# A chunked recurrence in front of two dense layers: stores, copies and products of the run-up in other places

## Chip, cores, metric

One NeuronCore of one Trainium2 chip runs the whole program in one launch. The metric is the device time of one execution in microseconds (us), lower is better. All data are float32.

## What is computed

Six arrays r, k, v, w, a, b of shape batch 4, heads 8, sequence 768, width 40 drive a recurrence; each of the 32 (batch, head) pairs has a 40x40 state, zero at first. Its result goes through two dense layers:

```python
for t in range(S):
    y[:, :, t] = np.einsum('bhd,bhde->bhe', rt, state)
    Sa = np.einsum('bhde,bhe->bhd', state, at)
    state_decay = state * wt[:, :, None, :] - np.einsum('bhd,bhe->bhde', Sa, bt)
    state = state_decay + np.einsum('bhd,bhe->bhde', vt, kt)
# x = y as [4, 768, 320]
h = relu(x @ w_in); c = conv3_along_sequence(h, conv_w)      # d_ff 1024
x = (h * sigmoid(c)) @ w_out
h = relu(x @ w2_in); u, v = halves(h)                        # 512 each
out = (u * (w_spatial @ layernorm(v) + b_spatial)) @ w2_out
```

## The kernel before, in words

The recurrence is worked in blocks. The sequence is cut into six groups n = 0 to 5 of 128 steps, each of two chunks of 64. A unit kk (0 to 23) is one batch i in one group n; a pair p (0 to 11) is two batches of one group, so it holds units 2p and 2p+1. All loads are made by pairs. The third to sixth pair of the change are pairs 2 to 5.

**The decay.** `lam_prep(n)` (line 55) makes for groups n and n+1 the running products of w (`lam`, 40 scans forward on VectorE, line 73) and their reciprocals (`ilam`, a reciprocal and 40 scans backward, line 79). Both are stored to DRAM scratch (`put`, line 65, four stores per kind, 320 KB each) and read back pair by pair in another layout. `l0`, `l2` and `l4` are these generators for groups 0|1, 2|3 and 4|5. The source of the `ilam` of groups 2 and 3 lies in a buffer of the tag "G", which later holds a pair's G tile.

**Loading a pair.** `l_araw`, `l_ln`, `l_P`, `l_il` (lines 101 to 134) issue loads on SyncE's queue (SP): a, lam (tile `lnA`), the packed b|k (tile `P`) and ilam (tile `il`, two copies of 64x16x40 into the lower half; one buffer for most pairs). `l_g` (line 121) multiplies a by lam into the tail of the pair's G tile on GpSimd (POOL); `l_ar` (line 126) copies it to `AR` on ScalarE (ACT); `l_dup` (line 138) copies the lower half of `il` to the upper half on ACT; `l_pm` (line 145) multiplies `P` by `il` on VectorE (DVE). `loadZ` (line 310) loads v|r of a pair (tile `ZU`, three buffers shared with the decay tiles of `l0`, `l2` and `l4`), `loadV` (line 315) copies v from it on ACT.

**One unit.** `A(kk)` transposes `AR` (line 157, TensorE), masks it on ACT (`bdA`, 159), transposes `P` (167), copies that to `PT` on ACT (168), multiplies the two (174) and masks the result into G on DVE (175). When the second unit of a pair is done, G's diagonal blocks are stored to `tb` (181, four stores). `subst(n)` loads them as `L` (189), inverts them by substitution on DVE (198 to 208), copies the result to `LT` (211) and stores `dt` and `dd` (213, 214); `loadD(p)` loads these back (226, 227 or 229). `Bp(kk)` builds the inverse of the whole chunk (lines 244 to 296), `Cp(kk)` carries the state through both chunks (327 to 342), `Dp(kk)` makes the output (360 to 385).

**What sets the order.** The program is written out by hand for SP, DVE and ACT: each executes its instructions in the order in which the Python emits them. Ahead of the loop (lines 420 to 466) the emission is a plain list of calls. `mixed(kk,g,m)` emits A(kk) with m scans of the generator g in its middle; `steps(g,m)` emits m steps of a generator; `drain` the rest. `later(m,f)` puts f off by m ticks, `flush()` emits everything put off. In the loop, unit kk does its C and D, B of the next unit and A of the unit nine ahead in slots given by `ORDER`; each slot is a tick, and the table `SCHED` says in which slot the loads of a coming pair stand. The first pass (kk = 0) has offsets of its own (lines 497, 498). `L4T` is the tick at which the eight `lam` and `ilam` stores of groups 4 and 5 are emitted. The numbers of steps stand in `W`. After the recurrence come the two layers (lines 788 to 922), which the change leaves alone.

Of the kernel before, what the change touches and what calls it, by code (L numbers as in the profile page):

```python
# [11 lines left out]
def attention(tc, keep, ident, vr,bk,w,a, x, spare=None):  # L12
# [4 lines left out]
    with ExitStack() as ctx:  # L17
# [36 lines left out]
        lms={}; BQ=[sy]  # L54
# [32 lines left out]
        def later(m,f):  # L87
            due.append((now[0]+m,f)); 
# [4 lines left out]
        def flush():  # L93
            while due: tick()
# [6 lines left out]
        def l_araw(p):  # L101
            if p>=NK//2: return
            n,j,u,s0,bs,xs=part(p)
            t=u['a']=sb.tile([128,H2,D],F32,name="araw",tag="VM",bufs=6) if p<4 else sb.tile([128,H2,D],F32,name="araw",bufs=1)
            sy.dma_start(out=t,in_=a[n,j])
# [5 lines left out]
        def l_P(p):  # L111
            if p>=NK//2: return
            n,j,u,s0,bs,xs=part(p)
            P=u['P']=sb.tile([128,H2,2,D],F32,name="P",bufs=6)
            sy.dma_start(out=P,in_=bk[n,j].rearrange("q t x c e -> (q t) x c e"))
        def l_g(p):
            if p>=NK//2: return
            n,j,u,s0,bs,xs=part(p)
            u['AR']=sb.tile([64,H2,2,D],F32,name="AR",bufs=2)
            G=u['G']=keep.tile([128,H2,2*C+D],F32,name="G",bufs=5)  # L120
            G_.tensor_tensor(G[:,:,2*C:],u['a'],u['lnA'],ALU.mult)
        def l_ar(p):
            if p>=NK//2: return
            n,j,u,s0,bs,xs=part(p)
            for c in range(2):
                AC.copy(u['AR'][:,:,c],u['G'][c*C:(c+1)*C,:,2*C:])
            u['ok1']=True
# [7 lines left out]
        def l_dup(p):  # L135
            if p>=NK//2: return
            n,j,u,s0,bs,xs=part(p)
            AC.copy(u['il'][64:128],u['il'][0:64])
            u['ok3']=True
        def l_pm(p,eng=None):  # L140
            if p>=NK//2: return
            n,j,u,s0,bs,xs=part(p)
            assert u['ok3']
            for hs in (slice(0,H),slice(H,H2)) if p==0 else (slice(0,H2),):
                (eng or G_).tensor_tensor(u['P'][:,hs],u['P'][:,hs],u['il'][:,:,hs].rearrange("p c h e -> p h c e"),ALU.mult)
            u['ok2']=True
# [256 lines left out]
        def drain(g):  # L403
            for _ in g: pass
# [4 lines left out]
        with tc.manual_schedule(engines={mybir.EngineType.SP,mybir.EngineType.DVE,mybir.EngineType.Activation}):  # L409
            flat=lambda t: t.rearrange("p h e -> p (h e)")[:,0:512]  # L410
            def both(g,f):

                for _ in g:
                    yield
                    next(f,None)
            def steps(g,m):
                for _ in range(m): next(g,None)
            def mixed(kk,g,m):
                A_=A(kk); steps(A_,3); steps(g,m); drain(A_)
            l0=lam_prep(0); next(l0); next(l0)  # L420
            il12={p:sb.tile([128,2,H2,D],F32,name="il2",tag="P",bufs=6) for p in (1,2)}
            l_araw(0); l_P(0)
            l2=lam_prep(2); next(l2); next(l2)
            steps(l0,D+1); lms['lam',0](); l_P(1)
            l_ln(0); l_ln(1); l_araw(1)
            l_g(0); l_ar(0); l_g(1)
            drain(l0); lms['ilam',0]()
            l_il(0); l_il(1)
            lms['lam',1](); lms['ilam',1]()
            warm(flat(pair[0,0]['lnA']),WARM0); warm(flat(pair[0,1]['lnA']),WARM1)  # L430
            l_ar(1); l_dup(0)
            l_P(2); l_araw(2); l_ln(2); l_il(2)
            steps(l2,W[0]); l_pm(0,V)
            a0=A(0); next(a0); warm(flat(pair[0,1]['lnA']),WARM2)
            steps(a0,2); l_dup(1); steps(l2,W[1]); drain(a0)
            l_pm(1,V)
            mixed(1,l2,W[2]); flush()
            lam_end(0)
            l4=lam_prep(4); next(l4); next(l4)
            mixed(2,l2,W[3]); mixed(3,l2,W[4]); flush()  # L440
            s0=subst(0); next(s0)
            l_P(3); l_araw(3); l_ln(3); l_il(3)
            l_g(2); l_ar(2); l_dup(2)
            drain(l2); l_pm(2,V)
            mixed(4,l2,0); steps(l4,W[11])
            steps(s0,W[5])
            mixed(5,s0,W[6]); flush()
            lms['lam',2](); lms['lam',3]()
            drain(s0); flush()
            loadD(0)  # L450
            loadZ(0); lms['ilam',2]()
            l_g(3); l_dup(3); l_ar(3); steps(l4,W[7]); l_pm(3,V)
            mixed(6,l4,W[8]); mixed(7,l4,W[8])
            l_P(4); l_araw(4); l_ln(4); flush()
            sub1=subst(1); next(sub1)
            lms['ilam',3](); l_il(4)
            b0=Bp(0)
            for _ in range(4): next(b0); steps(l4,W[9])
            loadV(0)
            drain(b0); drain(l4)  # L460
            later(7,lambda: (l_g(4),l_ar(4),l_dup(4))); later(10,lambda: l_pm(4,V))
            bg.append(sub1)
            def l4done():
                for f in ('lam','ilam'):
                    for z in (4,5): lms[f,z]()
            later(L4T,l4done)
            with tc.manual_schedule():
                none=iter(()); acc=0.0; dg={}
                def staging(z):
                    def tmp():  # L470
                        mo=sb.tile([128,2,512],F32,name="mo",tag="bdA",bufs=1)
                        return [sb.tile([128,512],I32,name="ct",tag="PT",bufs=2),mo[:,0],mo[:,1]]
                    return (lambda: sb.tile([128,512,2],I32,name="raw",tag="AR",bufs=2)),tmp
                later_layer=spare(FC=512,staging=staging) if spare else none
                done=0
                ex=lambda kk: EX[kk-14] if kk>=14 else 0
                for kk in range(NK):
                    i,n=units[kk]
                    ahead=[z for z in (EARLY[kk] if kk<len(EARLY) else [kk+LA] if kk+LA<NK-2 or not LAST2 else [NK-2,NK-1] if kk+LA==NK-2 else []) if z<NK]
                    gens={'A':chain(*[A(z) for z in ahead]),'B':Bp(kk+1) if kk+1<NK else none,'C':Cp(kk),'D':dg.pop(kk-1) if kk else none}  # L480
                    gens['Z']=dg[kk]=Dp(kk)
                    if kk==6 or kk==14: lam_end(n+1)
                    po=(kk+LA)//2 if (kk+LA+1)%2 else (kk+LA+1)//2
                    z=-1
                    for g in ORDER if kk<TAIL else ORDER2:
                        if g=='W':
                            warm(ident,WM)
                            continue
                        z+=1
                        for _ in range(max(1,len(ahead)) if g=='A' else 1): next(gens[g],None)  # L490
                        if z in BX and kk+1<NK and units[kk+1][1] in SMALL: next(gens['B'],None)
                        while done<ex(kk-1)+(ex(kk)-ex(kk-1))*(z+1)//19:
                            next(later_layer,None); done+=1
                        tick(); acc+=RATE0 if kk<3 else RATE if kk<14 else RATE2; pump(int(acc)); acc-=int(acc)
                        for s,f in SCHED[(kk+LA+1)%2]+SCHEDC[kk%2]:
                            if s==z:
                                if f=='il' and kk==0: later(12,lambda po=po: l_il(po))
                                elif f=='Z' and kk==0: later(18-z,lambda kk=kk: loadZ(kk//2+1))
                                elif f=='Z': loadZ(kk//2+1)
                                elif f=='V': loadV(kk//2+1)  # L500
                                else: {'araw':l_araw,'ln':l_ln,'P':l_P,'g':l_g,'ar':l_ar,'il':l_il,'pm':(lambda p: l_pm(p,V)) if PMV else l_pm,'dup':l_dup}[f](po)
                    if any(z%4==3 for z in ahead): nxt=subst(ahead[-1]//4 if ahead[-1]%4==3 else ahead[0]//4); ll=LL if kk+LA<NK-2 else LL2; later(ll,lambda z=nxt: next(z)); later(ll+SUB,lambda z=nxt: bg.append(z))
                pump(1000)
                for _ in dg.pop(NK-1): next(later_layer,None)
                flush()
# [5 lines left out]
ORDER2="DCCDDBCBACDADDABBAA"  # L511
ORDER="CDCBDDCBDDACABBDAAA"
LA=9
L4T=4
RATE=1.25
RATE2=1.25
RATE0=1.4
# [13 lines left out]
SMALL=(0,)  # L531
BX=(0,9)
DTLS=2
W=[34,9,9,12,12,8,8,12,8,9,4,10]
EX=[3, 7, 7, 9, 11, 15, 19, 22, 26, 28]


# [527 lines left out]
```

## Time and profile before

| | us |
|---|---|
| median of 3 runs | 969.81 |
| lowest, highest | 964.55, 976.65 |
| the profiled execution | 971.86 |
| its span, first to last instruction | 970.1 |

The rows further down come from the profiled execution; times in them are microseconds from the start of its span. A row of the timeline has the start, the duration, the engine, the source line, the operation, what it writes and reads, how many instructions are merged in it, and in square brackets how long the engine was idle before and what ended that. PE is the matmul side of TensorE. SPq rows are the issue of a DMA, not its transfer. PEclk is the granted TensorE clock as a share of 2.4 GHz, so 0.50 is 1.2 GHz.

### The profile page before, as it was taken

How to read it: one execution, taken by the hardware profiler on the slowest of the kernel's cores; microseconds unless marked ns; L12 is line 12 of the kernel's file. 1: busy time of each engine (PE TensorE's matmuls, PEld its weight loads, DVE VectorE, ACT ScalarE, POOL GpSimd, SP SyncE). 2: the span in 40 equal slices, each digit the busy share in tenths (PEclk: the TensorE clock that was granted, in tenths of full speed). 3: DMA queues.
4: the chain of work that ended last, by engine and by line, in shares of the span. 5: the costliest groups of instructions: out<-in, count | busy, mean ns of one | idle time of the engine just before them, and what ended most of it. 6: DMA issues, size and time to landing. Idle time of an engine off the chain costs nothing. (4 is left out here: it accounts for less than half of the span.)

```text
span 970.1 us, 23472 instructions
## 1 busy us (share of the span) xinstructions
PE 869.4 (90%) x9575; PEld 799.8 (82%) x9575; DVE 662.0 (68%) x1503; ACT 535.8 (55%) x1166; POOL 204.2 (21%) x268
## 2 busy tenths in 40 slices
PE   0876579999999999989988889998999999998997
PEld 0565569899998998888877779997899889998997
DVE  6876738387695886866659977368743877268841
ACT  0452547777778776457756655266534654266521
POOL 2100000111112102023320011234222441234321
PEclk9975669999999999779979899999999999999999
DMA  9978773555745537144331230111011100011001
GB/s 217 206 163 188 206 156 73 153 109 114 163 112 144 119 73 177 40 127 122 96 103 54 85 105 8 45 51 46 1 32 55 34 22 25 22 51 31 1 2 45
DMA packets 149189, 86.70 MB, mean 89 GB/s; under 512 B 124176, under 2 KB 138256, under 8 KB 147152
## 3 DMA queue, kind: packets, MB, share of 16 engines
q1 hardware_dynamic: 148800, 84.78, 35.2%
q8 instruction: 77, 1.26, 0.5%
q14 instruction: 40, 0.33, 0.1%
q10 hardware_dynamic: 272, 0.33, 0.1%
HBM read 61.24 MB, written 23.86 MB: 88 GB/s over the span
## 5 line engine op out<-in xcount | busy, mean ns | idle before, releaser
L688 PE MATMUL psp<-spt,vv 128*128 128x384 f32 x576 | 105.6, 338 | 0.5 <-DVE vv L816 0.3
L688 PE MATMUL ph<-XT,G 128*128 128x386 f32 x512 | 102.6, 346 | 0.7 <-DVE XT L721 0.7
L688 PEld LDWEIGHTS psp<-spt,vv 128*128 128x128 f32 x576 | 100.2, 188 | 2.2 <-ACT vv L813 1.1
L688 PEld LDWEIGHTS ph<-XT,G 128*128 128x128 f32 x512 | 93.8, 194 | 1.1 <-DVE XT L721 1.0
L764 PE MATMUL acc<-gh,G 128*128 128x384 f32 x320 | 71.3, 349 | 16.0 <-ACT gh L748 9.3
L750 POOL TENSOR_TENSOR gl<-c,gh 128x384 fp32r<-128x384 f32 x48 | 66.3, 1381 | 89.8 <-ACT gh L748 78.2
L331 POOL COPY ZU<-ZU 64x320 f32<-64x320 f32 x48 | 24.9, 520 | 259.9 <-ACT ZU L329 259.8
L764 PEld LDWEIGHTS acc<-gh,G 128*128 128x128 f32 x320 | 56.5, 192 | 24.5 <-ACT gh L748 13.2
L174 PE MATMUL p<-PT,bdA 80*128 80x128 f32 x384 | 59.6, 315 | 10.6 <-ACT PT L168 10.3
L174 PEld LDWEIGHTS p<-PT,bdA 80*128 80x128 f32 x384 | 54.8, 223 | 14.9 <-ACT PT L168 14.7
L833 DVE TENSOR_TENSOR psp<-psp,bb 128x384 f32<-128x384 f32 x32 | 18.1, 566 | 70.6 <-PE psp L688 70.5
L206 DVE TENSOR_TENSOR tmp<-L 128x30 f32<-128x30 f32 (+9 forms) x150 | 57.6, 384 | 6.5 <-DMA L<-tb 2.5
L746 DVE TENSOR_TENSOR c<-h,c 128x384 f32<-128x384 f32 x64 | 39.3, 614 | 33.2 <-ACT c L743 32.9
L748 ACT CAST gh<-c 128x384 fp32r<-128x384 f32 x64 | 32.9, 514 | 52.4 <-DVE c L746 51.0
L373 PE MATMUL pS<-bdR,ZV 80*128 80x128 f32 x384 | 56.7, 292 | 4.0 <-ACT ZV L367 2.4
L208 DVE TENSOR_TENSOR L<-L,tmp 128x30 f32<-128x30 f32 (+9 forms) x150 | 53.0, 353 | 3.9
L175 DVE TENSOR_TENSOR G<-p,mT 128x512 f32<-128x512 f32 x48 | 32.8, 688 | 32.7 <-PE p L174 32.1
L837 ACT CAST zh<-u 128x384 fp32r<-128x384 f32 x28 | 14.4, 513 | 73.2 <-DVE u L834 73.2
L295 PE MATMUL pw<-bdN,G 128*104 128x128 f32 x384 | 53.6, 300 | 0.9 <-issue 0.9
L381 PE MATMUL py<-P,SS 128*64 128x40 f32 x768 | 52.1, 240 | 2.0 <-DVE SS L374 1.6
L373 PEld LDWEIGHTS pS<-bdR,ZV 80*128 80x128 f32 x384 | 49.0, 199 | 5.8 <-ACT ZV L367 2.8
L295 PEld LDWEIGHTS pw<-bdN,G 128*104 128x104 f32 x384 | 50.2, 192 | 1.5 <-issue 1.0
(185 smaller groups left out, 2095.3 us busy)
## 6 DMA issues: line engine op xcount, KB each, us to landing
P<-in_bk_dram SPq DMA_DIRECT2D x12, 640.0 KB, 5.7
ZU<-in_vr_dram SPq DMA_DIRECT2D x12, 640.0 KB, 6.9
lq<-in_w_dram SPq DMA_DIRECT2D x12, 320.0 KB, 6.5
araw<-in_a_dram SPq DMA_DIRECT2D x12, 320.0 KB, 6.5
lam<-lq SPq DMA_DIRECT2D x12, 320.0 KB, 4.5
lnA<-lam SPq DMA_DIRECT2D x12, 320.0 KB, 6.9
ilam<-lq SPq DMA_DIRECT2D x12, 320.0 KB, 5.3
il<-ilam SPq DMA_DIRECT2D x24, 160.0 KB, 4.2
```

Source lines behind the costliest of these rows:

```text
L174: T.matmul(p3[:,j],lhsT=bdA[:,g*4+j].rearrange("p c t -> p (c t)"),rhs=PTs[g][:,j],start=True,stop=True)
L175: V.tensor_tensor(G[:,hs,0:2*C],p3,mT.rearrange("p a t -> p (a t)").unsqueeze(1).to_broadcast([128,4,2*C]),ALU.mult)
L206: V.tensor_tensor(t,L[:,j+1:HB,j:j+1].to_broadcast([128,m,j]),L[:,j:j+1,0:j].to_broadcast([128,m,j]),ALU.mult)
L208: V.tensor_tensor(L[:,j+1:HB,0:j],L[:,j+1:HB,0:j],t,ALU.add)
L295: T.matmul(p[:104,j],lhsT=G[:,h0+g*4+j,C:],rhs=N[:,g*4+j],start=True,stop=True)
L373: T.matmul(p[:,j].rearrange("p c t -> p (c t)"),lhsT=ZV[:,j,0:2*C],rhs=bdR[:,j].rearrange("p c t -> p (c t)"),start=True,stop=True)
L381: T.matmul(py[c*C:(c+1)*C,h],lhsT=SS[:,j,c],rhs=P[:,h0+h,c],start=True,stop=False)
L688: L.tc.nc.tensor.matmul(out,lhsT=l,rhs=r,start=start and i==0,stop=stop and i==len(prs)-1)
L746: V.tensor_tensor(c,h[:,1:TH+1],c,ALU.mult)
L748: AC.copy(gh,c)
L750: def low(v): v.tensor_tensor(gl,c,gh.bitcast(F32),ALU.subtract)
L764: nc.tensor.matmul(acc[m],lhsT=l,rhs=r,start=f==0 and z<5 and z in (0,1,3),stop=f==NF-1 and z>=5)
```

## The change

All of it lies ahead of the loop and in its first pass. No instruction is added or left out; the order on TensorE stays the same.

- Pair 2: `l_dup(2)` comes before the A of unit 3, and `l_pm(2)` comes before the last five scans of `l2`.
- Pair 3: `l_dup(3)`, `l_pm(3)` and `l_ar(3)` come right after the A of unit 5, ahead of the rest of the substitution of group 0, of its `dt` and `dd` and of twelve scans of `l4`.
- Decay stores of groups 2 and 3 (`lam`) are issued before the first `tb` stores of group 1; those of groups 4 and 5 (`lam` and `ilam`) at tick 14 and not 4.
- Pair 4: `l_il(4)` is issued before the second `tb` stores of group 1; `l_g`, `l_ar`, `l_dup` come two ticks earlier, `l_pm(4)` too.
- Pair 5: `l_il(5)` comes three ticks earlier, `l_dup(5)` six ticks later. `loadZ(1)` comes six ticks later.

```diff
-            mixed(2,l2,W[3]); mixed(3,l2,W[4]); flush()
+            mixed(2,l2,W[3]); l_dup(2); l_g(2); mixed(3,l2,W[4]); flush()
             s0=subst(0); next(s0)
             l_P(3); l_araw(3); l_ln(3); l_il(3)
-            l_g(2); l_ar(2); l_dup(2)
-            drain(l2); l_pm(2,V)
+            lms['lam',2](); lms['lam',3]()
+            l_ar(2); l_pm(2,V); drain(l2)
             mixed(4,l2,0); steps(l4,W[11])
+            l_g(3)
             steps(s0,W[5])
             mixed(5,s0,W[6]); flush()
-            lms['lam',2](); lms['lam',3]()
+            l_dup(3); l_pm(3,V); l_ar(3)
             drain(s0); flush()
             loadD(0)
             loadZ(0); lms['ilam',2]()
-            l_g(3); l_dup(3); l_ar(3); steps(l4,W[7]); l_pm(3,V)
-            mixed(6,l4,W[8]); mixed(7,l4,W[8])
-            l_P(4); l_araw(4); l_ln(4); flush()
+            l_P(4); l_araw(4); l_ln(4)
+            mixed(6,l4,W[7]); mixed(7,l4,W[8])
+            l_il(4); flush()
             sub1=subst(1); next(sub1)
-            lms['ilam',3](); l_il(4)
+            lms['ilam',3]()
...
-            later(7,lambda: (l_g(4),l_ar(4),l_dup(4))); later(10,lambda: l_pm(4,V))
+            later(5,lambda: (l_g(4),l_ar(4),l_dup(4))); later(8,lambda: l_pm(4,V))
...
-                                if f=='il' and kk==0: later(12,lambda po=po: l_il(po))
-                                elif f=='Z' and kk==0: later(18-z,lambda kk=kk: loadZ(kk//2+1))
+                                if f=='il' and kk==0: later(9,lambda po=po: l_il(po))
+                                elif f=='dup' and kk==0: later(6,lambda po=po: l_dup(po))
+                                elif f=='Z' and kk==0: later(24-z,lambda kk=kk: loadZ(kk//2+1))
...
-L4T=4
+L4T=14
...
-W=[34,9,9,12,12,8,8,12,8,9,4,10]
+W=[34,9,9,12,12,8,8,6,8,9,4,10]
```

On DVE around the product of pair 3 (L145; L175 are the masks of a unit's A, L198 and L200 the substitution, L73 the scans of `l4`), before:

```order
L175 TENSOR_TENSOR G<-p_669,mT 128x4x128
L175 TENSOR_TENSOR G<-p_675,mT 128x4x128
L198 TENSOR_TENSOR tmp<-L 128x108
...
L200 TENSOR_TENSOR L<-L,tmp 128x2x14
L210 MEMSET L 128x32
L211 COPY LT<-L 128x1024
L73 SCALAR_TENSOR_TENSOR lq<-lq,zer 128x64 x12
L145 TENSOR_TENSOR P<-P,il 128x1280
L73 SCALAR_TENSOR_TENSOR lq<-lq,zer 128x64 x8
```

and now:

```order
L175 TENSOR_TENSOR G<-p_676,mT 128x4x128
L175 TENSOR_TENSOR G<-p_682,mT 128x4x128
L145 TENSOR_TENSOR P<-P,il 128x1280
L198 TENSOR_TENSOR tmp<-L 128x108
...
L200 TENSOR_TENSOR L<-L,tmp 128x2x14
L210 MEMSET L 128x32
L211 COPY LT<-L 128x1024
L73 SCALAR_TENSOR_TENSOR lq<-lq,zer 128x64 x6
```

The product now stands right behind the masks of unit 5, ahead of the twelve operations that were left of the substitution.

On SP from the load of unit 0's inverse (L226, L227) on, where lam_110 and lam_111 are the `lam` of groups 2 and 3, lam_112 of group 4, ilam_116 and ilam_117 the `ilam` of groups 2 and 3, before:

```order
L227 DMA D_706<-dd_126 128x16x32
L310 DMA ZU<-in_vr_dram 64x2560
L67 DMA ilam_116<-lq_155 32x2560 x2
L115 DMA P<-in_bk_dram 128x1280
L105 DMA araw<-in_a_dram 128x640
L110 DMA lnA<-lam_110 128x16x40
L181 DMA tb_121<-G 32x16x32 x4
L189 DMA L<-tb_121 128x1024
L67 DMA ilam_117<-lq_155 32x2560 x2
L134 DMA il<-ilam_116 64x16x40 x2
L67 DMA lam_112<-lq 32x2560 x2
```

and now:

```order
L110 DMA lnA<-lam_110 128x16x40
L134 DMA il<-ilam_116 64x16x40 x2
L181 DMA tb_121<-G 32x16x32 x4
L189 DMA L<-tb_121 128x1024
L67 DMA ilam_117<-lq_155 32x2560 x2
L226 DMA DT<-dt_132 128x16x32
L227 DMA D_1173<-dd_126 128x16x32
L134 DMA il<-ilam_116 64x16x40 x2
L105 DMA araw<-in_a_dram 128x640
L110 DMA lnA<-lam_110 128x16x40
L67 DMA lam_112<-lq 32x2560 x2
```

The `il` of pair 4 moved ahead of the `tb` stores and of the load of `L`, and the eight stores of groups 4 and 5 moved behind the loads of pair 5.

On ACT from unit 1's B to unit 9's A (L126 and L138 are `l_ar` and `l_dup`; the first pair of them is pair 4, the later L138 is pair 5), before:

```order
L329 COPY ZU<-pu 64x4x40 x2
L126 COPY AR<-G 64x16x40 x2
L138 COPY il<-il 64x1280
L275 COPY F<-pf 32x256 x2
L287 COPY bdN<-px 32x8x32 x2
L159 ACTIVATE bdA<-p_1244,mB 80x8x64 x2
L168 COPY PT<-p_1256 80x512
L168 COPY PT<-p_1281 80x512
L296 ACTIVATE WT<-pw 104x512 x2
L138 COPY il<-il 64x1280
L159 ACTIVATE bdA<-p_1329,mB 80x8x64 x2
```

and now:

```order
L126 COPY AR<-G 64x16x40 x2
L138 COPY il<-il 64x1280
L329 COPY ZU<-pu 64x4x40 x2
L275 COPY F<-pf 32x256 x2
L287 COPY bdN<-px 32x8x32 x2
L159 ACTIVATE bdA<-p_1236,mB 80x8x64 x2
L168 COPY PT<-p_1248 80x512
L168 COPY PT<-p_1276 80x512
L296 ACTIVATE WT<-pw 104x512 x2
L159 ACTIVATE bdA<-p_1328,mB 80x8x64 x2
```

The copies of pair 4 moved ahead of the state copy L329, and the copy of pair 5 left its place ahead of unit 9's mask L159.

## Rows read from the trace of the kernel before

**Rows 1.** The page: the span of the profiled execution.

```profile
span 970.1 us, 23472 instructions
```

**Rows 2.** Stretches: length, busy (instructions) of PE PEld DVE ACT POOL, PEclk, DMA share, GB/s.

```profile
56.00:72.00 16.00, 12.25 (x57) 10.54 (x56) 10.51 (x34) 7.44 (x12) 1.56 (x1) 0.57 0.68 159
...
119.60:131.00 11.40, 11.31 (x112) 10.03 (x112) 7.24 (x17) 4.58 (x9) 0.00 (x0) 0.69 0.90 207
131.00:138.30 7.30, 0.09 (x1) 0.00 (x0) 0.69 (x2) 3.04 (x5) 1.53 (x1) 0.67 0.94 222
138.30:147.00 8.70, 8.70 (x149) 7.90 (x153) 3.34 (x7) 4.97 (x13) 0.51 (x1) 0.50 0.22 36
...
160.00:350.00 190.00, 187.57 (x3420) 172.09 (x3421) 138.12 (x323) 140.91 (x306) 32.11 (x52) 0.99 0.56 125
```

**Rows 3.** Timeline from unit 3's product to unit 4's transposes.

```profile
53.42 2.05 PE L174 MATMUL p<-PT,bdA 80*128 80x128 f32 x16 [0.88 <-ACT PT L168]
...
56.12 1.16 DVE L79 TENSOR_TENSOR_SCAN lq<-lq,zer 128x64 f32<-128x64 f32 x5
...
58.81 1.90 PE L167 MATMUL p<-ident,P 128*80 128x128 f32 x8 [2.77 <-DVE P L145]
```

**Rows 4.** Timeline from unit 5's masks to unit 0's B.

```profile
72.73 1.28 DVE L175 TENSOR_TENSOR G<-p,mT 128x512 f32<-128x512 f32 x2
...
77.24 1.03 DVE L211 COPY LT<-L 128x1024 f32<-128x1024 f32 x1
...
80.40 1.48 DVE L145 TENSOR_TENSOR P<-P,il 128x1280 f32<-128x1280 f32 x1
...
82.03 1.90 PE L167 MATMUL p<-ident,P 128*80 128x128 f32 x8 [8.42 <-DVE P L145]
...
94.49 0.72 PE L244 MATMUL pe<-DT,G 32*16 32x16 f32 x64
```

**Rows 5.** Timeline of SP: the issue of five DMAs.

```profile
79.68 1.48 SPq L213 DMA_DIRECT2D dt<-LT  x1
...
87.66 0.37 SPq L226 DMA_DIRECT2D DT<-dt  x1
...
106.61 0.34 SPq L189 DMA_DIRECT2D L<-tb  x1
...
170.79 0.33 SPq L213 DMA_DIRECT2D dt<-LT  x1
...
174.47 0.37 SPq L226 DMA_DIRECT2D DT<-dt  x1
```

**Rows 6.** Line 67 from 107 to 108 us: its two stores, issue to landing.

```profile
DMA to landing us min/median/max: 4.2/5.1/6.0
```

**Rows 7.** Timeline ahead of unit 8's A.

```profile
113.81 0.59 ACT L329 COPY ZU<-pu 64x160 f32<-64x160 f32 x2 [1.95 <-PE pu L327]
...
114.88 1.52 POOL L121 TENSOR_TENSOR G<-araw,lnA 128x640 f32<-128x640 f32 x1
...
116.43 1.46 ACT L126 COPY AR<-G 64x640 f32<-64x640 f32 x2 [2.03 <-POOL G L121]
...
119.61 0.64 PE L284 MATMUL px<-F,X 32*32 32x32 f32 x3 [4.84 <-ACT F L275]
```

**Rows 8.** Timeline of unit 9's A, and of v's copy in the loop's second pass.

```profile
130.02 1.07 PE L167 MATMUL p<-ident,P 128*80 128x128 f32 x8
...
135.24 1.26 ACT L138 COPY il<-il 64x1280 f32<-64x1280 f32 x1 [5.98 <-DMA il<-ilam]
...
138.30 3.78 PE L174 MATMUL p<-PT,bdA 80*128 80x128 f32 x16 [7.21 <-ACT PT L168]
...
155.96 1.35 ACT L315 COPY VM<-ZU 64x640 f32<-64x640 f32 x2
```

**Rows 9.** The page's DMA issues: count, KB each, median us to landing.

```profile
lam<-lq SPq DMA_DIRECT2D x12, 320.0 KB, 4.5
...
il<-ilam SPq DMA_DIRECT2D x24, 160.0 KB, 4.2
```

## Prediction

> **What bounds the kernel now.** I first read the busy time by stretch. From 160 to 350 us TensorE is busy 187.57 of 190 us at a granted clock of 0.99, so in the loop there is nothing for the order of loads to win, and what is won ahead of it is carried to the end. In the run-up it is not so: 0.09 us of work between 131.0 and 138.3, and 12.25 of 16 us from 56 to 72 [rows 2]. I then followed the waits of TensorE there in the timeline and asked for each what ended it. Four are large: 2.77 us for the product of P and il on DVE [rows 3], 8.42 us for the same product one pair later [rows 4], 4.84 us for a copy on ACT that stands behind AR and il of pair 4 [rows 7], and 7.21 us for a copy on ACT that stands behind il of pair 5, itself 5.98 us late from DMA [rows 8]. The change moves an instruction out of the way at each of the four. So I forecast a gain. What I have to find out is how much of each is late for a second reason.
>
> **Unit 4.** The product of pair 2 ran behind five scans that start at 56.12. Put ahead of them it starts some 1.0 us earlier, and the transposes at 58.81 with it [rows 3]. The scans now lie in DVE's wait for unit 4. The il copy that moved ahead of unit 3's A lies in an idle stretch of ACT. Cost 0, at most its own 1.26 us [rows 8] if its load is late there.
>
> **Units 6 and 7.** The masks of unit 5 end at 72.73 + 1.28 = 74.0; with the microsecond from above, 73.0. The product of 1.48 us follows at once, so the transposes of unit 6 start at 74.6 and not at 82.03: 7.4 us earlier [rows 4]. The first matmul of unit 0's B came 94.49 - 82.03 = 12.5 us after them, hence 87.1. The rest of the substitution, pushed back by the product, took from 74.0 to 77.24 + 1.03 = 78.3, so 4.3 us: LT is ready at 74.5 + 4.3 = 78.8 instead of 78.3 [rows 4]. That is the price on DVE. It is hidden, if dt lands sooner: before, DT's load was issued 87.66 - 79.68 = 8.0 us behind the store of dt, with four decay stores just ahead in the queue; in a later group, with nothing ahead, 174.47 - 170.79 = 3.7 us [rows 5]. The decay stores are now some ten microseconds earlier, ahead of the tb stores. I take 3.7: DT's load goes out at 82.5, and has 4.6 us until the matmul wants it. The other end is 8.0: 86.9.
>
> **Group 1's L and pair 4.** These 7.4 us are not kept. The next wait is for data. Between DT's load and that of L stand on SP D1, ZU, two ilam, P, araw, lnA and four tb: with DT, by their shapes, 3,328 KB. They took 106.61 - 87.66 = 18.95 us [rows 5]. The change puts il of pair 4 (twice 160 KB) ahead of tb, so 3,648 KB: at the same pace 20.8 us, and L is issued at 82.5 + 20.8 = 103.3 and not 106.61. At the 222 GB/s of the best stretch [rows 2] it is 16.8 us, 99.3; with the slow dt it is 107.7.
>
> What follows L decides, and here the change adds a wait. The G of pair 4 takes the buffer from which ilam of group 3 is stored, so l_g(4) on POOL waits for those two stores, issued right behind L, 0.4 and 0.9 us later, and landing 4.2 and 6.0 us after that [rows 6]. Before, the state copy of unit 0's second chunk went ahead of AR on ACT (113.81); now it stands behind AR and il, and so do copy F, the matmuls px and TensorE's in-order rest. From L's issue: 0.9 + 6.0 for the store, 1.52 on POOL, 1.46 for AR, 1.26 for il, 0.59 for the state copy [rows 7, 8], about 0.4 for half of F: 12.1 us. Before it was 119.61 - 106.61 = 13.0 [rows 5, 7]. So px starts at 103.3 + 12.1 = 115.4, a gain of 4.2 us; 8.2 with the fast queue, nothing (-0.2) with the slow dt.
>
> At this place a page speaks against the change. The rows have il's 160 KB at 4.2 us from issue to landing and lam's 320 KB at 4.5 [rows 9]. The Trainium skill, "DMA: Bandwidth & Descriptors", section "Why small descriptors are slow", says that every packet carries a fixed overhead of about three cycles beside one per 32 bytes. By an estimate from that page the 160-byte pieces of il cost 8 cycles for 5, so il would count as 512 KB, L would be issued 1.1 us later, and the sum would be 11.1 instead of 12.2. The trace agrees in direction: half the bytes take nearly as long. The queue's own pace above holds lnA, of pieces just as small, so I keep the 20.8.
>
> **Unit 9.** The transposes of unit 9 end at 130.02 + 1.07 = 131.1, their product starts at 138.30 [rows 8]. Between them ACT waited 5.98 us for il of pair 5, copied it, and only then made the mask and PT. That copy now stands in the next pass. Without it the gap should be like that of unit 3, 0.88 us [rows 3]: 132.0, a gain of 6.3 us. If AR of pair 5, the next on ACT, or the state copy behind it took its place, TensorE would meet that only after the product; its loads are now ahead of the eight decay stores. Bounds: 4 to 6.6.
>
> **Clock.** From 138.3 to 147 TensorE was busy all 8.70 us at half clock, after the idle 7.3 us [rows 2]. With the gap closed I expect the higher level. The product of unit 9 took 3.78 us there, and 2.05 in unit 3 at full clock [rows 3, 8]: 1.7 us. The rest of the stretch hangs on ACT copies, to which il is now added; I count nothing for it. Bounds: 0, and half of 8.70, 4.3.
>
> **Sum.** 4.2 + 6.3 + 1.7 = 12.2 us. The profiled execution took 971.86 around its span of 970.1 [rows 1]; 971.86 - 12.2 = 959.7. It lies 2.05 above the median of 969.81, so on the median 957.6. The loads put back (P, tb, ZU behind eight decay stores) cost nothing as long as they land before their readers, which is the third rival.
>
> **Rivals.** *First, issued earlier but landing no earlier.* The queue is the limit from 79 to 106 us, and the change asks it for more ahead of tb. If dt lands as late as before, the 4.2 become -0.2; with a late il of pair 5 the 6.3 become 4 and the clock's term stays: 5.5 us, 964.3. For it: DMA share 0.90 and 0.94 in the busy stretches [rows 2]. Against it: the 3.7 us of dt in a free queue [rows 5].
>
> *Second, the clock stays up from px on.* The stretch from 119.6 to 131 had 0.69 on average, so some 7 of its 11.4 us were at half [rows 2]; 3.5 more, and 2.6 more for the whole of 8.70: 18.3 us, 951.5. The Trainium skill, "TensorE: Matmul & The Clock Gate", section "What's actually happening", has idleness halve the clock and activity release it; by that rule the shorter gaps give this rival's time. The trace bears it out at 131 to 147, but not from 58.81 to 71, where TensorE worked almost without a pause at half clock (0.57 on average from 56 to 72).
>
> *Third, v|r of the second pair comes too late, and the kernel is slower.* ZU(1) now stands behind il, araw and lnA of pair 5, eight decay stores, P and tb: 5,056 KB from the end of pair 4's product, about 115.9. At 207 GB/s [rows 2] it lands at 140.9, at the pace of the L queue at 144.7. Its reader, v's copy on ACT at 155.96 [rows 8], will stand at 143.8. Every microsecond beyond that holds ACT and then TensorE. It costs all 12.2 if the pace falls below 129 GB/s; at 90, half of the L queue's, ZU lands at 173.5: 987.3. Against it: no busy stretch of mine is that slow. A loss of a microsecond is well possible.
>
> **How the numbers follow.** My forecast (9 to 16 us gained) gets 0.62, the first rival 0.18, the second 0.17, the third 0.03. The range of 947 to 966 takes in nearly all of the first two rivals. Faster by over 2%, which is about what a measurement of this kernel can tell from no change, needs 19.4 us: the far part of the second rival and luck of the runs, 0.12. Slower by over 2%: part of the third, 0.01. Within 2%: 0.87.
>
> **What would show it.** In the new trace the transposes of unit 6 should start near 74.6 and B's first matmul near 87; L's issue near 103; px near 115, with AR's idle time before it ended by POOL, and POOL's by ilam; the product of unit 9 within a microsecond of its transposes, near 128, at full clock soon after. The prediction is wrong if L's issue stays near 106, if v's copy on ACT waits for the load of ZU, or if TensorE shows new pauses between 140 and 200 us.

## The result and the profile after

| | before | after |
|---|---|---|
| median of 12 runs each, us | 973.81 | 960.22 |
| lowest, highest, us | 964.55, 983.17 | 955.54, 962.56 |
| the profiled execution, its span, us | 971.86, 970.1 | 955.54, 953.8 |

The ratio after to before is 0.9882, with a 95% interval from 0.9847 to 0.9916. It leaves out two slow runs of the kernel before, at 980.85 and 983.17 us. The means of the others are 971.2 and 959.7 us, a gain of 11.5 us (8.2 to 14.9); the medians of all runs differ by 13.6. Forecast were 12.2.

The stretches of the kernel after, in the columns of [rows 2]:

```profile
119.60:131.00 11.40, 10.52 (x169) 9.66 (x168) 9.89 (x20) 7.09 (x16) 2.23 (x2) 0.96 1.03 258
131.00:138.30 7.30, 6.18 (x177) 5.49 (x173) 5.00 (x11) 6.85 (x17) 0.45 (x1) 0.94 0.76 173
138.30:147.00 8.70, 8.70 (x106) 8.24 (x106) 8.08 (x19) 4.41 (x8) 0.00 (x0) 0.50 0.89 186
```

TensorE now works 6.18 of 7.30 us from 131.0 to 138.3, where it worked 0.09. From 138.3 to 147 it works without a break at half clock, as before, though on other work.

To see what the loop keeps I use one mark in all runs: the last of the 16 copies of v by L315 ahead of 350 us. The line's summary, before and after (count, duration in ns, first to last start):

```profile
L315 ACT COPY VM<-ZU x16: 718/722/727, 103.0 to 347.2; 64x640 f32<-64x640 f32 x16
```

```profile
L315 ACT COPY VM<-ZU x16: 717/722/727, 96.5 to 335.4; 64x640 f32<-64x640 f32 x16
```

The mark moves from 347.2 to 335.4, by 11.8 us. The two profiled executions differ by 971.86 - 955.54 = 16.3 us; the other 4.5 arise behind the mark, where the change moves little. In a second profile of the changed kernel (run r9_after below) the mark stands at 335.9 in a span of 959.1 us. That leaves 623.2 us behind the mark, against 622.9 before and 618.4 in the first profile after, so the 4.5 are not the change's.

Then the places the prediction speaks of, in the timeline after. Units 4 to 7 and unit 0's B, as in [rows 3, 4]:

```profile
58.05 1.04 PE L167 MATMUL p<-ident,P 128*80 128x128 f32 x8 [1.70 <-DVE P L145]
...
71.47 1.26 ACT L138 COPY il<-il 64x1280 f32<-64x1280 f32 x1 [4.77 <-DMA il<-ilam]
...
72.75 1.46 ACT L126 COPY AR<-G 64x640 f32<-64x640 f32 x2
72.76 1.49 DVE L145 TENSOR_TENSOR P<-P,il 128x1280 f32<-128x1280 f32 x1 [1.18 <-ACT il L138]
...
74.27 1.07 PE L157 MATMUL p<-ident,AR 64*80 64x64 f32 x8 [4.44 <-ACT AR L126]
...
75.27 1.93 PE L167 MATMUL p<-ident,P 128*80 128x128 f32 x8
...
77.48 1.06 DVE L211 COPY LT<-L 128x1024 f32<-128x1024 f32 x1
...
87.76 0.73 PE L244 MATMUL pe<-DT,G 32*16 32x16 f32 x64
```

The product of pair 3 stands right behind the masks, but the transposes of unit 6 wait a little longer, for AR (4.44 us), which stands behind the il copy; that one waited 4.77 us for its load. SP, as in [rows 5], and what L's load releases:

```profile
78.57 0.34 SPq L213 DMA_DIRECT2D dt<-LT  x1
...
81.21 0.37 SPq L226 DMA_DIRECT2D DT<-dt  x1
...
101.60 0.34 SPq L189 DMA_DIRECT2D L<-tb  x1
...
107.33 0.20 DVE L206 TENSOR_TENSOR tmp<-L 128x30 f32<-128x30 f32 x1 [2.75 <-DMA L<-tb]
...
109.23 1.54 POOL L121 TENSOR_TENSOR G<-araw,lnA 128x640 f32<-128x640 f32 x1 [6.71 <-DVE tmp L206]
...
110.81 1.46 ACT L126 COPY AR<-G 64x640 f32<-64x640 f32 x2 [4.99 <-POOL G L121]
...
114.60 0.65 PE L284 MATMUL px<-F,X 32*32 32x32 f32 x4 [3.54 <-ACT F L275]
```

DT's load follows the store of dt after 2.64 us, not 8.0. L's load goes out 5.0 us earlier than before; px too. Here the profile puts POOL's wait for G down to a step of the substitution on DVE, not to a store. Unit 9 and the copy of v, as in [rows 8]:

```profile
126.39 2.05 PE L174 MATMUL p<-PT,bdA 80*128 80x128 f32 x16 [0.88 <-ACT PT L168]
...
143.63 1.35 ACT L315 COPY VM<-ZU 64x640 f32<-64x640 f32 x2
```

The gap of unit 9 is 0.88 us and its product runs at full clock. The copy of v waits for nothing.

### The profile page after: what moved, and what is told of

It is laid out like the page before. It is cut to its first block, busy times and chain, and to the rows that moved or that the text cites. A ratio compares the mean times of both kernels' runs of the same rounds, so it can differ in the third digit from the quotient of the medians.

```text
span 953.8 us, 23470 instructions
## 1 busy us (share of the span) xinstructions
PE 863.3 (91%) x9575; PEld 793.1 (83%) x9575; DVE 661.8 (69%) x1503; ACT 535.7 (56%) x1166; POOL 204.9 (21%) x268
## 3 DMA queue, kind: packets, MB, share of 16 engines
q8 instruction: 77, 1.26, 0.6%
## 5 line engine op out<-in xcount | busy, mean ns | idle before, releaser
L174 PE MATMUL p<-PT,bdA 80*128 80x128 f32 x384 | 57.3, 306 | 4.6 <-ACT PT L168 4.2
L174 PEld LDWEIGHTS p<-PT,bdA 80*128 80x128 f32 x384 | 52.6, 215 | 8.8 <-ACT PT L168 8.6
L383 PE MATMUL py<-ZV,bdR 80*64 80x40 f32 x768 | 51.1, 237 | 0.0
L840 POOL TENSOR_TENSOR zl<-u,zh 128x384 fp32r<-128x384 f32 x28 | 28.6, 1020 | 101.0 <-ACT zh L839 91.5
```

Of the source, the lines that this page charges most:

```text
L174: T.matmul(p3[:,j],lhsT=bdA[:,g*4+j].rearrange("p c t -> p (c t)"),rhs=PTs[g][:,j],start=True,stop=True)
L383: T.matmul(py[c*C:(c+1)*C,h],lhsT=bdR[:,j,c],rhs=ZV[:,j,2*C:],start=False,stop=True)
```

## The experiments

All are the changed kernel with one edit, except r2_loop (the kernel before with one half of the change). No run leaves out any part of the computation. Columns: issue of L's load of group 1, start of unit 1's px, start of unit 9's product and its gap, the mark, and the ratio of times to the kernel before with its interval. All but the last come from one profiled execution each. r3_ilam3 and r7_pm3 have two timed runs, so their ratios say little.

| run | L | px | unit 9 (gap) | mark | ratio |
|---|---|---|---|---|---|
| before | 106.61 | 119.61 | 138.30 (7.21) | 347.2 | 1 |
| after | 101.60 | 114.60 | 126.39 (0.88) | 335.4 | 0.9882 (0.9847 to 0.9916) |
| r9_after | 100.60 | 112.79 | 124.36 (0.88) | 335.9 | 0.9891 (0.9857 to 0.9925) |
| r1_front | 100.64 | 113.82 | 129.33 (3.79) | 342.1 | 0.9962 (0.9919 to 1.0005) |
| r2_loop | 107.23 | 120.28 | 132.46 (0.88) | 342.1 | 0.9953 (0.9922 to 0.9984) |
| r5_dup5 | 101.10 | 113.84 | 126.13 (1.26) | 335.4 | 0.9909 (0.9873 to 0.9944) |
| r11_copy | 103.25 | 115.77 | 128.28 (0.88) | 337.6 | 0.9888 (0.9838 to 0.9937) |
| r7_pm3 | 100.76 | 113.26 | 124.98 (0.88) | 334.2 | 0.9894 (0.9798 to 0.9989) |
| r6_lam | 104.15 | 115.68 | 127.36 (0.88) | 336.5 | 0.9935 (0.9899 to 0.9971) |
| r4_il4 | 99.64 | 112.67 | 124.73 (0.88) | 333.7 | 0.9922 (0.9888 to 0.9957) |
| r3_ilam3 | 101.96 | 110.24 | 122.86 (0.88) | 330.3 | 0.984 (0.9753 to 0.9927) |
| r10_ilam3 | 101.54 | 109.90 | 121.32 (0.88) | 330.3 | 0.9885 (0.9854 to 0.9915) |
| r8_both | 100.55 | 110.91 | 123.76 (0.88) | 333.6 | 0.9852 (0.9779 to 0.9925) |
| r12_sub | 102.39 | 109.36 | 122.20 (0.88) | 333.3 | 0.9843 (0.9802 to 0.9885) |

**r9_after: how far the points move by themselves.** The kernel after, unaltered.

> The changed kernel once more, unaltered, to see how far its points move from one execution to the next. If what comes ahead of 140 us is set by the order of the queue, L's load goes out at 101.6 within 0.7, px starts at 114.6 within 1, and the mark stands at 335.4 within 1; time 1.2% below the kernel before. Rival (the clock's changes are at other points each time, and the mark with them): px within 1, the mark off by 2 or more.

L's load 1.0 and px 1.8 us earlier, the mark 0.5 later. Both theories are partly wrong: px moves by more than 1, and what px gained is lost again behind unit 9. So a px that differs by under 2 us, or a mark by under 2 or 3, is no finding here.

**r1_front and r2_loop: the two halves.** r1_front takes back the loop's half, as below; r2_loop makes the reverse edit in the kernel before:

```diff
-                                if f=='il' and kk==0: later(9,lambda po=po: l_il(po))
-                                elif f=='dup' and kk==0: later(6,lambda po=po: l_dup(po))
-                                elif f=='Z' and kk==0: later(24-z,lambda kk=kk: loadZ(kk//2+1))
+                                if f=='il' and kk==0: later(12,lambda po=po: l_il(po))
+                                elif f=='Z' and kk==0: later(18-z,lambda kk=kk: loadZ(kk//2+1))
...
-L4T=14
+L4T=4
```

> The half ahead of the loop alone: il copy of pair 5, its load, the next v|r and the decay stores of groups 4 and 5 are back in their old places. The mark for all runs is the start of the last of the 16 copies of v by L315: 347.2 us in the kernel before, 335.4 in the changed one, 11.8 earlier. Theory (the terms add up): px moves to 114.6 as in the changed kernel, unit 9 waits for il of pair 5 as before, so the mark moves by the first term alone, 5.0, to 342.2; time 0.5% below the kernel before. Rival (the first term is lost again, since the load of il of pair 5 is issued no earlier and ACT meets it at the same 135 us): mark 346 to 347, no gain.

> The kernel before with the loop's half alone: il copy of pair 5 six ticks later and in the next pass, its load at 9 instead of 12 ticks, v|r of the second pair at 24, the decay stores of groups 4 and 5 at 14 ticks. Theory (the terms add up): px stays at 119.6, the product of unit 9 starts 0.9 us behind its transposes, at 132.0, the mark moves by the rest, 11.8 - 5.0 = 6.8, to 340.4; time 0.7% below the kernel before. Rival (this half is the whole gain, because the loop waits for pair 5 in any case): mark 336 to 337.

Each half moves the mark by 5.1 us; together they give 11.3 to 11.8. That r1_front meets the 342.2 of its first theory is luck. The wait for il of pair 5 shrinks by itself, since with px earlier the decay stores ahead of it leave from 102.0 on, not from 111.1:

```profile
126.27 1.26 ACT L138 COPY il<-il 64x1280 f32<-64x1280 f32 x1 [2.57 <-DMA il<-ilam]
...
129.33 3.79 PE L174 MATMUL p<-PT,bdA 80*128 80x128 f32 x16 [3.79 <-ACT PT L168]
```

The product starts 9.0 us earlier than before, not 5.0, and of these the mark keeps 5.1. The product at half clock is not the reason, for it was so before too (3.78 us). The rest goes with a second stretch at half clock, in r1_front from 159 to 172.5, in the kernel before only from 174.4 to 177.8. The windows around it, r1_front and then before, columns as in [rows 2]:

```profile
158.00:173.00 15.00, 15.00 (x182) 13.83 (x179) 3.40 (x9) 8.17 (x17) 0.45 (x1) 0.54 0.31 82
```

```profile
174.00:178.00 4.00, 4.00 (x24) 3.83 (x22) 0.98 (x2) 2.00 (x4) 0.00 (x0) 0.57 0.67 103
```

So the two halves add up at the mark by chance; at unit 9's product they gain 9.0 and 5.8 us, both together 11.9. The times of r1_front fall in two groups, five from 955.8 to 960.2 us and five from 965.1 to 969.9 with the profiled one among them, and the interval of its ratio includes 1. What brings the second stretch on, no run tests. In r2_loop the gap closes as forecast, but px is 0.7 us later than before and the mark 1.7 short of the theory, inside the spread.

**r5_dup5 and r11_copy: the load of il of pair 5 or its copy.** r5_dup5 takes away the new line for `dup`, so the copy is back in its old place; r11_copy keeps that line and makes the rest of r1_front's edit.

```diff
-                                elif f=='dup' and kk==0: later(6,lambda po=po: l_dup(po))
```

> The changed kernel with the il copy of pair 5 alone back in its old place in pass 0, ahead of the mask and PT of unit 9; its load stays early, ahead of the eight decay stores. Theory of the prediction (the copy stood in ACT's way, and by it TensorE lost the wait for the load): the load is issued near 115 and lands near 120, so the copy waits for nothing and costs its own 1.26 us and little more: mark 336.7 to 337.5. That would say that the place of the load is worth more than that of the copy. Rival (the place of the copy is the whole second term): mark 342.

> The changed kernel with the load of il of pair 5, the v|r of the second pair and the decay stores of groups 4 and 5 back in their old places; the copy of il of pair 5 alone keeps its new one, in the next pass. Theory (either the early load or the late copy is enough to free unit 9): the load lands near 126 as in the run with the half ahead of the loop alone, its copy at 132 waits for nothing, the gap of unit 9 is 0.88 us and the mark 335 to 336. Rival (the late load shows at the next reader, the P product of pair 5 ahead of unit 10): mark 337 or later.

The timeline of r5_dup5, then of r11_copy:

```profile
123.06 1.26 ACT L138 COPY il<-il 64x1280 f32<-64x1280 f32 x1
...
126.13 2.05 PE L174 MATMUL p<-PT,bdA 80*128 80x128 f32 x16 [1.26 <-ACT PT L168]
```

```profile
134.37 1.26 ACT L138 COPY il<-il 64x1280 f32<-64x1280 f32 x1
...
139.85 1.48 DVE L145 TENSOR_TENSOR P<-P,il 128x1280 f32<-128x1280 f32 x1
```

With the load early, the copy in its old place waits for nothing and lengthens the gap by 0.38 us, the mark by nothing. With the load late, the copy in its new place waits for nothing either, nor does the product of pair 5 behind it; the mark is 2.2 us later than after, of which 1.2 are in px already, and the rest is within the spread. The rival's number came out, its wait did not. Either edit alone frees unit 9; the second adds at most 0.4.

**r7_pm3: pair 3 back behind the substitution.**

```diff
-            l_dup(3); l_pm(3,V); l_ar(3)
             drain(s0); flush()
...
+            l_ar(3); l_dup(3); l_pm(3,V)
             l_P(4); l_araw(4); l_ln(4)
```

> The changed kernel with AR, il copy and P product of pair 3 back behind the whole substitution of group 0, and all else in its new place. Theory (what is won at unit 6 is not kept, the queue sets L's load): the transposes of unit 6 start near 80 and not at 75.3, B's first matmul near 92, L's load stays within a microsecond of 101.6, mark 335.0 to 336.4. Rival (TensorE's chain through units 6 and 7 sets the tb stores and so L): mark later by the full 4 us, 339 to 340.

```profile
78.56 1.90 PE L167 MATMUL p<-ident,P 128*80 128x128 f32 x8 [6.36 <-DVE P L145]
...
91.02 0.73 PE L244 MATMUL pe<-DT,G 32*16 32x16 f32 x64
...
100.76 0.34 SPq L189 DMA_DIRECT2D L<-tb  x1
...
106.81 1.54 POOL L121 TENSOR_TENSOR G<-araw,lnA 128x640 f32<-128x640 f32 x1 [1.26 <-DMA ilam<-lq]
```

Units 6 and 7 and B are 3.3 us later than after, L's load and px are not, and the mark is 334.2. Of the largest single step of the prediction's chain, 7.4 us forecast and 6.8 measured at unit 6, the run takes back these 3.3, and by themselves they are worth nothing. The row of G names here what the profile after did not: POOL waits for a store of ilam.

**r6_lam: the decay stores of groups 2 and 3 back ahead of dt.**

```diff
-            lms['lam',2](); lms['lam',3]()
             l_ar(2); l_pm(2,V); drain(l2)
...
+            lms['lam',2](); lms['lam',3]()
             l_dup(3); l_pm(3,V); l_ar(3)
```

> The changed kernel with the four decay stores of groups 2 and 3 back behind the tb stores, just ahead of dt. Theory (the prediction's price for a slow dt): DT's load goes out some 8 us behind the store of dt, near 86.9 and not at 81.2, L's load near 107, px 4 us later or more; mark 339.6. Rival (the bytes are the same wherever they stand, and L's load is behind all of them in both): DT's load later by 3 to 5 us, L's load by less than 1, mark 335.4 to 336.5.

```profile
77.91 1.42 SPq L213 DMA_DIRECT2D dt<-LT  x1
...
84.10 0.37 SPq L226 DMA_DIRECT2D DT<-dt  x1
...
104.15 0.34 SPq L189 DMA_DIRECT2D L<-tb  x1
```

DT's load goes out 6.2 us behind the store of dt: less than the 8.0 priced, more than 2.64. L's load comes 2.6 to 3.6 us later than in the two profiles after, px 1.1 to 2.9, the mark 0.6 to 1.1. Neither theory holds whole: the rival is right on DT's load and the mark, wrong on L's. About half of the price is paid at the queue, and what reaches the mark is no more than the spread.

**r4_il4: il of pair 4 back behind L's load.**

```diff
-            l_il(4); flush()
+            flush()
             sub1=subst(1); next(sub1)
-            lms['ilam',3]()
+            lms['ilam',3](); l_il(4)
```

> The changed kernel with the two loads of il of pair 4 back behind tb, L's load and ilam of group 3. The prediction priced these loads ahead of tb at 1.8 us of L's issue. Theory (what holds px is AR, which waits for POOL's G and that for the stores of ilam): L's load goes out near 99.8 instead of 101.6, ilam of group 3 as much earlier, il itself lands near 107, ahead of its copy, px 1.8 us earlier, mark 333.6. Rival (il behind L is late for its copy and the copy stands ahead of the state copy and F): il lands behind 111, px no earlier or later than 114.6, mark 335 to 338.

From DT's load (80.82) to L's (99.64) it takes 18.8 us, 20.4 in the kernel after (81.21 to 101.60). So il costs 1.6 us there, or 1.2 against r9_after (80.60 to 100.60); 1.8 were priced, at the queue's pace by bytes. (By the estimate that the prediction weighed, from the rule on small pieces in the Trainium skill, "DMA: Bandwidth & Descriptors", section "Why small descriptors are slow (HBM only)", it would be 1.8 + 1.1 = 2.9; the measurement is nearer to bytes.) The copy is not late. px and mark agree with the first theory to 0.1 us against the first profile after, but against r9_after px is the same; that the time is won is not shown.

**r3_ilam3 and r10_ilam3: the wait of G taken away.** Both have the same edit; r10_ilam3 is timed longer, on one chip with r9_after, and the rows are its own.

```diff
-            loadZ(0); lms['ilam',2]()
+            loadZ(0); lms['ilam',2](); lms['ilam',3]()
...
-            lms['ilam',3]()
             b0=Bp(0)
```

> The changed kernel with the two stores of ilam of group 3 beside those of group 2, some 17 us earlier and no longer behind L's load. Theory (AR of pair 4 waits for POOL's G, and G for these stores): AR starts near 102 and not at 110.8, the state copy waits for its matmuls alone, px starts near 111.4 though L's load goes out 1.8 us later; mark 332.2. Rival (POOL's G waits for a copy of L on DVE, as the profile names it, or L itself sets px): AR stays behind 110, mark 335.4 to 337.

> The run with the stores of ilam of group 3 beside those of group 2, once more with more rounds, on the same chip as the changed kernel. Theory (AR's wait gone is a gain of some 4 us at px): px within 1 of 110.2, time some 0.4% or more below the changed kernel's, 1.6% or more below the kernel before. Rival (the further 1.2 us at the mark was the clock alone, and on the median nothing is left): ratio within 0.2% of the changed kernel's.

```profile
101.69 1.54 POOL L121 TENSOR_TENSOR G<-araw,lnA 128x640 f32<-128x640 f32 x1
...
105.12 1.46 ACT L126 COPY AR<-G 64x640 f32<-64x640 f32 x2
...
108.42 0.59 ACT L329 COPY ZU<-pu 64x160 f32<-64x160 f32 x2 [0.56 <-PE pu L327]
```

G and AR no longer wait, AR and il are done before the copy of the state (108.42), and px stands 2.6 to 4.7 us earlier than in the two profiles after; the mark is 330.3 in both runs, 5.1 to 5.6 earlier. So G did wait for the stores. AR starts at 105.1 and not near 102, behind other copies on ACT. In the times the gain does not show: a median of 957.13 us against 959.04 of r9_after, and ratios to the kernel before of 0.9885 and 0.9891, which is what the rival said. Each is uncertain by 0.3%, 3 us, so a gain of that size is not excluded either.

**r8_both and r12_sub: what comes next.** r8_both joins the edits of r4_il4 and r3_ilam3. r12_sub adds this to r3_ilam3:

```diff
-            bg.append(sub1)
+            later(4,lambda: bg.append(sub1))
```

> Both orders of the last two findings in one: il of pair 4 behind L's load, and the stores of ilam of group 3 beside those of group 2. Theory (the two waits, for L and for G, are separate): L's load goes out near 101, AR of pair 4 starts near 101, the copy of il near 107, px near 109.4; mark 330.3, time 1.7% below the kernel before. Rival (the copy of il, whose load is now last, holds ACT as G did): il lands behind 109, px 111.5 or later, mark 332.5 or more, no better than the run with il alone moved (333.6).

> The run with ilam of group 3 moved, and in it the substitution of group 1 starts four ticks later, so that the first instruction on L no longer stands ahead of the state update m on DVE. Theory (once AR is free, L's landing sets px through that instruction): the matmuls pu start near 104 and not at 107.65, the state copy stands behind AR and il on ACT at 107.9, px starts near 109.0, mark 329 to 330. Rival (m waits for its own matmuls, or ACT is not free earlier): px 110.2 as before, mark as in the run without this edit; the substitution ends later and px of later units with it.

```profile
108.60 1.26 ACT L138 COPY il<-il 64x1280 f32<-64x1280 f32 x1 [2.84 <-DMA il<-ilam]
```

```profile
99.47 6.25 DVE L79 TENSOR_TENSOR_SCAN lq<-lq,zer 128x64 f32<-128x64 f32 x21
...
105.74 0.49 DVE L340 TENSOR_TENSOR m<-pm,VM 40x320 f32<-40x320 f32 x1
...
106.91 0.94 PE L327 MATMUL pu<-VM,WT 104*64 104x40 f32 x16 [2.72 <-DVE VM L342]
...
132.99 0.55 PE L327 MATMUL pu<-VM,WT 104*64 104x40 f32 x12 [2.61 <-issue]
```

In r8_both il lands last and holds ACT for 2.84 us, as the rival says, but px (110.91) lies between both theories. The mark is that of r4_il4; TensorE pauses in this run for 0.80 and 2.40 us more behind unit 9, so the mark does not tell them apart. Nothing is won over r3_ilam3. In r12_sub the first step on L is out of the way, but the state update m now stands behind the scans of groups 4 and 5, which fill DVE until 105.7. The matmuls pu start at 106.91, not near 104: the theory of m falls. px, at 109.36, is near the value expected but within the spread of the 109.90 of r10_ilam3, and the mark is 3 us late, most of it in a pause of TensorE at 130.4 (the last section). Its ratio is the lowest but one, but the intervals overlap with that of the changed kernel, and no run is shown to be faster than it.

## Why the prediction was right, and where it was not

**The sum.** 12.2 us forecast, 11.8 and 11.3 at the mark of two profiles, 11.5 by the ratio of times. That it came out so near is in part luck. Against 4.2, 6.3 and 1.7 us the terms measure 5.0, 6.9 and -0.1 in the first profile and 6.8, 7.1 and -2.6 in the second: two forecast too small make up for the third. The forecast time of 957.6 us stood on a median of 969.81 before; in the later runs the medians are 973.81 and 960.22. The first rival falls with L's issue at 101.60 and 100.60, and v's copy did not wait for ZU, so the third rival had nothing to stand on.

**Units 4 to 7.** Transposes of unit 4 at 58.05 (57.8 forecast), of unit 6 at 75.27 (74.6), LT ready at 78.54 (78.8), DT's load at 81.21 (82.5), B's first matmul at 87.76 (87.1). The step that was incomplete is "the product of 1.48 us follows at once, so the transposes of unit 6 start at 74.6": the il copy was late by its own load and AR stood behind it. It cost 0.7 us where nothing hung on it: "these 7.4 us are not kept" holds, and r7_pm3 shows it.

**First term, 4.2.** Measured 5.0 in the first profile and 6.8 in the second. L's load went out at 101.60 and 100.60 (103.3 forecast): dt came back in 2.64 us, faster than any row before, and the queue's own pace was right (r4_il4: 18.8 us without il, 18.95 in [rows 5]). L's load to px took 13.0 and 12.2 us (12.1 forecast), with AR behind G and G behind the stores, as the prediction had it, though the profiles after put G's wait down to DVE. G started 7.6 and 6.8 us behind L's issue, 6.9 were priced; r3_ilam3 and r10_ilam3 show that this wait, which the change brought along, cost 2.6 to 4.7 us at px.

**Second term, 6.3.** From px to unit 9's product it took 18.69 us before, 11.79 and 11.57 after: 6.9 and 7.1. The gap fell from 7.21 to 0.88 us, 6.3 as forecast. The rest is the clock: it rose 5.8 us behind px and not 7.0, in the middle of one product of unit 8. That product before, then after:

```profile
125.08 1.79 PE L174 MATMUL p<-PT,bdA 80*128 80x128 f32 x8
```

```profile
120.07 1.22 PE L174 MATMUL p<-PT,bdA 80*128 80x128 f32 x8
```

The reason is half right: the prediction put the gain down to the copy's new place; r5_dup5 and r11_copy show that its load's new place does the same alone. That the loads stand ahead of the decay stores it named only as a cover. Nor are the first two terms independent: with the half ahead of the loop alone (r1_front) the gap already falls to 3.79.

**Third term, 1.7.** This one failed. The step is "With the gap closed I expect the higher level": the product did take 2.05 us and not 3.78, but the half clock was not avoided, it came later. It lasted from 133.4 to 147.1 us before, from 137.5 to 147.7 after and from 135.2 to 145.4 in r9_after, which, like the kernel before, has a further 3.4 us of it, from 162.5 on. Between unit 9's product and the mark that makes 12.2, 10.2 and 13.6 us at half clock. The stretch from the product of unit 9 to the mark, in one row for each kernel, before, after and r9_after, columns as in [rows 2]:

```profile
138.30:347.20 208.90, 206.47 (x3813) 189.58 (x3814) 150.91 (x348) 153.17 (x336) 33.07 (x54) 0.97 0.54 120
```

```profile
126.39:335.40 209.01, 206.06 (x3813) 188.98 (x3814) 152.08 (x351) 154.59 (x337) 33.12 (x54) 0.98 0.60 132
```

```profile
124.36:335.90 211.54, 207.53 (x3814) 190.51 (x3815) 152.05 (x352) 154.86 (x338) 33.28 (x54) 0.97 0.59 131
```

208.9, 209.0 and 211.5 us: nothing is given back there, and in r9_after 2.6 are taken, with TensorE idle for 4.0 us of the stretch and not 2.4. The second rival, the clock up from px on, is out with it. The kernel after behind px, from unit 9's product on, and behind the fall:

```profile
115.00:120.00 5.00, 5.00 (x62) 4.22 (x63) 2.76 (x9) 2.46 (x5) 0.38 (x1) 0.50 0.70 145
126.39:137.40 11.01, 9.89 (x285) 9.06 (x285) 8.05 (x19) 9.74 (x25) 0.54 (x2) 1.00 0.85 220
137.40:147.10 9.70, 9.70 (x112) 9.03 (x111) 8.99 (x21) 5.04 (x10) 0.39 (x1) 0.50 0.85 182
```

TensorE was busy 9.89 of 11.01 us ahead of the fall, and it stayed at half through 9.70 us without a break. By the rule named there (the Trainium skill, "TensorE: Matmul & The Clock Gate", section "What's actually happening"), where activity releases the clock, that much work should have held it up; the trace does not agree. Why the clock fell there stays open.

## What to carry to other kernels

When a wait is removed on one engine, follow the data and not the engine: the next limit in this run-up was the DMA queue three times (il of pair 3, L of group 1, the stores of ilam), and 3 us won on TensorE ahead of a load from that queue were worth nothing. Look for stores that hold a buffer which a later step takes: such a wait need not show under its own name, and here moving the store was worth 5 us at the mark, though the times did not show it. A gap that closes need not bring the clock back: here the half clock only came later. And before two halves of a change are added up at a mark, look whether the clock ran alike in both.

## What was not expected of the hardware

TensorE stops within the 16 matmuls pu of unit 1's second chunk, after four of them, in the changed kernel (0.80 us) and in seven of the runs (up to 2.61 us, in r12_sub above). The profile names nothing that it waits for ("issue"). In the kernel before and in five of the runs, r3_ilam3 and r10_ilam3 among them, it does not stop there. The pause goes with two things: a packet of the instruction queue close by, and data on the DMA engines at the time. The DMA queues over 3 us in r12_sub (129 to 132), r10_ilam3 (126 to 129) and r1_front (139 to 142), where the 16 matmuls start at 130.06, 129.18 and 140.90 (packets, MB, share of the 16 engines):

```profile
q1 hardware_dynamic: 2025, 0.47, 72.9%
q8 instruction: 1, 0.02, 1.8%
```

```profile
q1 hardware_dynamic: 108, 0.61, 90.4%
q8 instruction: 1, 0.02, 2.1%
```

```profile
q8 instruction: 1, 0.02, 1.8%
```

In all eight profiles with the pause such a packet falls between 2.0 us ahead of the first of the 16 matmuls and 0.5 us behind it, and in the 3 us around it the data queue takes 57 to 88% of the engines. The longest pause has the latest packet. In r3_ilam3, r7_pm3 and r10_ilam3 the packet comes earlier, 2.3 to 3.0 us ahead; in the kernel before, r1_front and r11_copy there is next to no data beside it. That the pause is a fetch of instructions held up behind data is a guess from this, which no run tests. With two executions of one kernel 1.8 us apart at px, and with stretches at half clock that lie elsewhere in each, such pauses are a reason why gains of a microsecond or two ahead of the loop could not be told from nothing.
